# RWKV-5 attention with a SmeLU feed-forward on one core: another order of all steps, and the last copy in one piece

## The chip, the core and the metric

The kernel runs on one core of a Trainium2 chip. A core has five engines that run side by side and wait for one another by semaphores: TensorE (PE in the profile; its weight loads are listed as PEld), VectorE (DVE), ScalarE (ACT), GpSimd (POOL) and SyncE (SP), which here only issues DMAs. Transfers between the device's memory, the on-chip memory SBUF and again SBUF are carried by 16 DMA engines. Matmuls write into PSUM, a small memory of eight banks. The metric is the time of one execution in device microseconds. The kernel before took 175.04 us, the median of three runs (174.94 to 175.53).

## The reference

The first half is a linear attention with a decaying state, with batch 4, 8 heads, 768 steps and 48 columns per head; the second a feed-forward layer on 3072 tokens, 384 to 2048 to 384.

```python
for t in range(S):
    cur = einsum('bhd,bhe->bhde', u * k[t], v[t])
    y[t] = einsum('bhd,bhde->bhe', r[t], state + cur)
    state = w * state + einsum('bhd,bhe->bhde', k[t], v[t])
x = y.transpose(0, 2, 1, 3).reshape(B * S, H * D)
h = x @ w_in
g = where(h >= 1, h, where(h <= -1, 0, (h + 1) ** 2 / 4))
out = g @ w_out
```

## The kernel before

The 768 steps are cut into 6 chunks of 128. A unit n is one chunk of one batch row, 24 in all; a pair g holds units 2g and 2g+1, 12 in all. Within a chunk the recurrence is done by matmuls on scaled copies of K and R; from chunk to chunk a state of each batch row is carried on.

The steps for a pair g are these, each named as in the order below. `load.K.g`, `load.R.g` and `loadV.g` fetch inputs (SP; for g of 0 and 1 each in two halves, `.0` and `.1`). `V` casts V to bf16 (ACT). `Ks` and `Rs` scale K and R by powers of the decay, `KU` and `RKU` make the products for the u term, `usum` sums them per head, and `V2` scales V by that sum; most of these run on POOL. For the first three pairs `T` transposes Ks and Rs on PE and `TT` copies the result out of PSUM; for later pairs `KRT` transposes by DMA. `A` multiplies them, and `AT` masks A to the past. That is one masked product on DVE, or for two early units a cast on ACT and a mask on POOL. `Y` is the attention output (PE), and `y` adds V2 to it (DVE). `Sp` is a chunk's share of the state; `Tm` (DVE) adds the old state, `decay` (POOL) multiplies by the decay of a chunk, and `sbf` (ACT) makes a bf16 copy. `X` and `xT` transpose y: for the first three pairs on PE with a copy on ACT, later by DMA.

The feed-forward layer takes a pair's 256 tokens in four quarters q of 512 columns. `mm1.g.q` is 12 matmuls into a PSUM buffer h (three of these are shared with `A` and `T`). `relu` and `square` (ACT) and `gate` (DVE) compute the activation, and `mm2.g.j.q` is four matmuls that add unit j's share of that quarter into one of two PSUM banks. `o` copies the sum out, and `out` stores it. `w_in` (two pieces) and `w_out` (four) are weight loads that cast to bf16, issued by POOL on its own DMA queue.

What sets the order is one text, ORDER, written out by hand or by a search: a loop at the end of the kernel goes through its words, and each word issues one step. In `KU.0.1@D` the letter behind @ names the engine (D is DVE, P is POOL, A is ACT), and digits behind a colon name the buffers that the step takes. A number behind ~ puts so many idle matmuls ahead of a step, and `warm` is idle matmuls alone. Each engine runs its own instructions in the order of the text; SP's and POOL's DMA issues stand in theirs. A step that takes a buffer waits until its last reader is done. The line numbers of the profile that the text below uses: 210 copies and casts, 288 and 292 the weight loads, 302 the input loads, 325 Ks and Rs, 335 KU, 342 RKU, 367 V2, 404 A, 419 the mask, 444 Y, 479 decay, 516 mm1, 534 the gate, 544 mm2, 558 and 559 the last copy.

Of the kernel before, what the change touches and what calls it, by code (L numbers as in the profile page):

```python
# [43 lines left out]
relu.0.1:1 mm1.1.1.-1:0 gate.0.0:0 square.0.1:1 Tm.4@D:1 mm1.0.2.-1:2 relu.1.1:0 Y.5:1 square.1.1:0 V2.2.0@P:0 w_out.1
y.4:1 gate.0.1:1 w_out.2 X.4:0 w_out.3 mm1.0.3.-1:1 xT.4@A:2 gate.1.1:2 relu.0.2:1 Sp.3:0 y.5:2 mm1.1.0.-1:0
square.0.2:1 Tm.3@D KU.3.0@P:1 decay.4 gate.0.2:3 relu.0.3:0 relu.1.0:1 mm2.0.0.0:1 mm2.0.1.0:0 Ks.3.0@P:0 RKU.3.0@D:1
square.1.0:0 KRT.K.3:0 mm1.1.3.-1:2 mm2.0.1.1 Rs.3.0@P:0 mm2.0.0.1 square.0.3:1 gate.1.0:4 mm2.0.1.2 gate.0.3:5
# [580 lines left out]
```

## Time and profile before

| | |
|---|---|
| median of the runs | 175.04 us (174.94 to 175.53) |
| the profiled execution | 175.03 us, span 173.3 us |
| PE busy | 163.5 us, 94% |
| DVE, ACT busy | 134.8 and 134.9 us, 78% each |
| POOL busy | 118.1 us, 68% |
| share of the span on the last chain | PE 71%, DMA 10%, DVE 9%, ACT 5% |
| moved by DMA | 28.78 MB in 106,967 packets, most of them under 512 bytes |

The profile is one execution on the chip. Its parts are busy time by engine, the span in 40 slices, DMA queues (q1 has the transfers that SP issues, q0 those of POOL), the chain of work that ended last, groups of instructions with the idle time ahead of them and what ended it, and DMA issues with the time to landing. PE's busy time counts the depth of the pipeline, so a full PE is read from the idle time between instructions rather than from the share. Times are counted from the span's start.

### The profile page before, as it was taken

To read this page: it belongs to the slowest core of one execution; us is meant where nothing else is said; L and a number is where in the kernel's file an instruction comes from. 1 tells how busy PE (TensorE), PEld (TensorE's weight loads), DVE (VectorE), ACT (ScalarE), POOL (GpSimd) and SP (SyncE) were. 2 spreads that over 40 slices of the span, in tenths; PEclk is the share of its full clock that TensorE was granted. 3 is DMA by queue.
4 is the path that set the end of the run, shared out by engine and by line. 5 is a ranking of instruction groups with operands and counts; after the bars stand their busy time and mean duration, and the time that the engine had idled before them with its cause. 6 is when DMAs were issued, how large, how long until landed. Compare 5 with 4: busy or idle time off the path is not lost.

```text
span 173.3 us, 4141 instructions
## 1 busy us (share of the span) xinstructions
PE 163.5 (94%) x1674; PEld 123.7 (71%) x1674; DVE 134.8 (78%) x168; ACT 134.9 (78%) x194; POOL 118.1 (68%) x96
## 2 busy tenths in 40 slices
PE   7998789998999999979999999999999999999991
PEld 5786578765787866577786868876878868787650
...
GB/s 110 224 223 198 223 185 232 201 173 206 240 175 200 246 159 255 154 186 238 183 235 182 210 213 155 232 229 253 229 77 95 106 2 4 128 8 95 0 91 91
DMA packets 106967, 28.78 MB, mean 166 GB/s; under 512 B 100930, under 2 KB 106180, under 8 KB 106948
## 3 DMA queue, kind: packets, MB, share of 16 engines
...
q0 software_dynamic: 2912, 3.15, 11.3%
...
q14 instruction: 6, 0.05, 0.1%
...
## 4 chain that ended last, share of the span: by engine, by line
PE 71%; DMA 10%; DVE 9%; ACT 5%; issue 2%; POOL 1%; SPq 1%; DVEq 0%; POOLq 0%
PE hp L516 33%; PE op L544 30%; DMA VF<-in_v_dram 5%; DVE AT L419 3%; DMA xT<-yy 3%; PE A L404 3%; DVE RKU L342 2%; DMA K<-in_k_dram 2%; DVE gt L534 2%; PE Y L444 2%; PE Y L439 2%; PE Sp L430 1%; ACT V L210 1%; ACT RKU L353 1%; POOL V L367 1%
## 5 line engine op out<-in xcount | busy, mean ns | idle before, releaser
L516 PE MATMUL hp<-xT,w_in_sb 128*128 128x256 bf16 (+1 forms) x600 | 70.8, 268 | 2.7 <-DVE gt L534 1.0
L544 PE MATMUL op<-w_out_sb,gt 128*128 128x384 bf16 x384 | 71.7, 326 | 0.0
L534 DVE SCALAR_TENSOR_TENSOR gt<-sq,hp 128x1024 bf16<-128x1024 f32 x48 | 57.9, 1216 | 14.6 <-ACT sq L529 14.3
L516 PEld LDWEIGHTS <-w_in_sb 128*128 128x128 bf16 x600 | 55.8, 98 | 12.8 <-issue 2.9
L524 ACT ACTIVATE pt<-hp 128x1024 f32<-128x1024 f32 x48 | 48.6, 1017 | 13.5 <-PE hp L516 13.3
L529 ACT ACTIVATE sq<-pt 128x1024 f32<-128x1024 f32 x48 | 50.4, 1057 | 3.0 <-DVE gt L534 1.8
L544 PEld LDWEIGHTS <-gt 128*128 128x128 bf16 x384 | 35.6, 98 | 19.7 <-issue 0.2
L419 DVE TENSOR_TENSOR AT<-A,umask 128x1024 bf16<-128x1024 f32 x22 | 26.5, 1218 | 1.8 <-PE A L404 1.5
L367 POOL TENSOR_TENSOR V<-V,diag 128x768 f32<-128x768 bf16 (+1 forms) x12 | 16.5, 1375 | 9.1 <-ACT V L210 7.1
L335 POOL TENSOR_TENSOR KU<-K,u_bc 128x768 f32<-128x768 f32 (+1 forms) x13 | 21.3, 1640 | 1.9 <-DVE u_bc L210 1.8
L342 POOL TENSOR_TENSOR RKU<-R,KU 128x768 f32<-128x768 f32 (+1 forms) x13 | 20.7, 1595 | 0.3
L325 POOL TENSOR_TENSOR Ks<-Wdn,K 128x768 bf16<-128x768 f32 x10 | 18.3, 1828 | 2.1 <-PE Y L444 1.7
L479 POOL TENSOR_TENSOR state<-Tm,wCm 128x384 f32<-128x384 f32 x16 | 16.1, 1008 | 5.1 <-DVE Tm L466 5.1
L325 POOL TENSOR_TENSOR Rs<-Wup,R 128x768 bf16<-128x768 f32 x10 | 18.3, 1830 | 0.0
L458 DVE TENSOR_TENSOR yy<-Y,V 128x384 bf16<-128x384 f32 x18 | 9.9, 553 | 5.0 <-PE Y L444 3.5
L210 ACT CAST V<-VF 128x768 bf16<-128x768 f32 (+1 forms) x14 | 10.2, 736 | 2.7 <-DMA VF<-in_v_dram 2.7
L466 DVE TENSOR_TENSOR Tm<-Sp,state 128x384 f32<-128x384 f32 x16 | 8.9, 553 | 4.3 <-PE Sp L430 3.4
L444 PE MATMUL Y<-V,AT 128*128 128x48 bf16 x192 | 11.2, 184 | 1.1 <-POOL AT L414 0.7
L210 ACT COPY oo<-op 128x384 f32<-128x384 f32 x13 | 6.2, 475 | 7.6 <-PE op L544 7.5
L444 PEld LDWEIGHTS <-AT 128*128 128x128 bf16 x192 | 9.5, 96 | 2.7 <-POOL AT L414 1.0
L355 DVE TENSOR_REDUCE diag<-RKU 128x16 f32<-128x768 f32 (+1 forms) x13 | 11.0, 850 | 0.0
L210 ACT CAST state_bf<-state 128x384 bf16<-128x384 f32 x20 | 10.0, 504 | 0.0
...
## 6 DMA issues: line engine op xcount, KB each, us to landing
...
w_in_sb<-in_moe_w_in_dram POOLq DMA_DIRECT2D x2, 768.0 KB, 8.3
...
```

The lines of the kernel that those rows point to most:

```text
L210: nc.scalar.copy(out, in_) if e == "A" else engines[e].tensor_copy(out, in_)
L325: engines[e].tensor_mul(of_unit(dst, j0, j1)[:, :, :, :D], rep(tab, j1 - j0), of_unit(tiles[what, g], j0, j1))
L335: engines[e].tensor_mul(of_unit(tiles["KU", g], j0, j1), of_unit(tiles["K", g], j0, j1), rep(u_bc, j1 - j0))
L342: engines[e].tensor_mul(of_unit(tiles["RKU", g], j0, j1), of_unit(tiles["R", g], j0, j1), of_unit(tiles["KU", g], j0, j1))
L367: engines[e].tensor_mul(tiles["V2", g][:, hs, :], tiles["V", g][:, hs, :], tiles["diag", g][:, hs].unsqueeze(2).to_broadcast([P, hs.stop - ...
L419: nc.vector.tensor_mul(t.rearrange("p i n t -> p (i n) t"), tiles.pop(("A", n)).rearrange("p i n t -> p (i n) t"), umask.unsqueeze(1).to_b ...
L444: nc.tensor.matmul(t[:, 2 * p + i, :], tiles["AT", n][:, i, p, :], tiles["V", g][:, j * H + 2 * p + i, :], start=(c == 0), stop=True, skip ...
L516: nc.tensor.matmul(hp[:, f, cols], w_in_sb[:, i, n0 : n0 + P], tiles["xT", g][:, units, i, :], start=(i == 0), stop=(i == nK - 1), skip_gr ...
L524: nc.scalar.activation(tiles["pt", g, q], tiles["hp", g, q], AF.Relu, bias=0.5, scale=0.5)
L529: nc.scalar.activation(tiles["sq", g, q], tiles.pop(("pt", g, q)), AF.Square, bias=0.0)
L534: nc.vector.scalar_tensor_tensor(out=gt, in0=tiles.pop(("sq", g, q)), scalar=1.0, in1=tiles.pop(("hp", g, q)), op0=ALU.min, op1=ALU.max)
L544: nc.tensor.matmul(tiles["op", g, j], tiles["gt", g, q][:, f, j * P : (j + 1) * P], w_out_sb[:, n, :], start=(n == 0), stop=(n == nF - 1),)
```

## The change

All words of ORDER are put into another order, some with other engines, buffers and counts of idle matmuls. Those that change engines are u_bc, TT.2 and TT.4 (from DVE to ACT), usum.1.0 (ACT to DVE), KU.0.0 and KU.0.1 (exchanged between POOL and DVE), and nine of the copies o. The step `o` of the last unit copies its 384 columns on ACT in one piece; before, ACT copied 192 and DVE 192. Its store stays in two halves, on SP's queue and on ACT's. `W_OUT = 4` makes the number of pieces of w_out a constant with the slices it had, and `FUSE`, an empty list, adds a form of y that no pair takes.

The core of the diff, with the lines of ORDER that hold V.1.1, and those with w_in.0:

```diff
+W_OUT = 4
+FUSE = ()
...
-RKU.0.1@P T.2:2~9 TT.0@A:0 usum.0.0@D:0 Ks.1.1@D Ks.0.1@D KU.1.1@P Wup Sp.0:0 TT.2@D:1 A.0:1 V.0.1@A load.R.2.0:2
-AT.0.1:0 RKU.1.1@P Tm.0@D Sp.1:1~5 T.1:2 Tm.1@D w_in.0 V.1.0@A:1 A.2:1 Rs.1.1@D loadV.1.1 Sp.2:0 AT.0.0 TT.1@D:2
-usum.1.0@A:1 A.1:0~8 V2.0.0@P:0 Ks.2.0@P:2 AT.2.0:1 loadV.2.0:0 V2.1.0@A:1 Y.0:1 T.3:2 sbf.0@A Tm.2@D usum.0.1@D Y.2:0
...
-load.R.3.0:0 V.1.1@A X.1:1 Y.3:0 AT.5.0:0 A.4:0 V2.1.1@P xT.1@A mm1.0.0.1 V.2.0@A:2 Sp.5:1 y.3:0 RKU.2.0@P:0
...
+Rs.1.0@D:1 loadV.1.1 T.2:2 RKU.1.0@P:1 usum.0.0@D:0 Rs.0.1@D RKU.0.1@P V2.0.0@P:0 Tm.0@D V.1.0@A:1 Ks.0.1@D Ks.1.1@D
+A.0:1 Sp.2:0 KU.1.1@P TT.2@A:1 RKU.1.1@P Tm.2@D Rs.1.1@D usum.1.0@D:1 w_in.0 A.2:2 AT.2.0:0 sbf.0@A AT.0.1:1 AT.0.0
...
+Rs.2.0@P:2 y.0:0 Y.2:0 A.3:0 V.1.1@A Sp.3:1~4 V.0.1@A y.2:1 V2.0.1@A Sp.1:0 usum.1.1@D Tm.3@D warm.9.h.1 T.5:2 X.2:1
...
     def w_out_go(e, bk, i):
-        n = slice(i * FG, (i + 1) * FG)
+        n = slice(i * nF // W_OUT, (i + 1) * nF // W_OUT)
...
-            half = DO // 2
-            t = tiles["last", g, j] = [buf(bk[0], [P, half], F32, f"o_last{i}") for i in range(2)]
-            nc.scalar.copy(t[0], src[:, :half])
-            nc.vector.tensor_copy(t[1], src[:, half:])
+            t = tiles["last", g, j] = buf(bk[0], [P, DO], F32, "o_sb")
+            nc.scalar.copy(t, src)
...
-            for i, (queue, t) in enumerate(zip((nc.sync, nc.scalar), tiles.pop(("last", g, j)))):
-                queue.dma_start(out=rows[:, j, i * half : (i + 1) * half], in_=t)
+            t = tiles.pop(("last", g, j))
+            for i, queue in enumerate((nc.sync, nc.scalar)):
+                cols = slice(i * half, (i + 1) * half)
+                queue.dma_start(out=rows[:, j, cols], in_=t[:, cols])
```

Further on, the words from pair 4's A to its first mm1 read like this, before and after (other words left out): `A.9 A.8 mm2.2.1.2 mm2.3.0.0 mm2.2.1.3 mm2.3.0.1 Y.8 mm2.3.0.2 Y.9 mm2.3.0.3 A.11 A.10 mm2.3.1.0 Sp.10 mm2.3.1.1 mm2.3.1.2 Sp.9 mm2.3.1.3 mm1.4.0`, and now `A.9 A.8 mm2.2.0.2 mm2.2.1.1 mm2.2.0.3 mm2.2.1.2 mm1.3.1 Sp.8 mm2.2.1.3 mm1.3.2 Y.8 Y.9 mm1.3.3 mm2.3.0.0 mm2.3.1.0 mm2.3.0.1 mm2.3.1.1 mm2.3.0.2 A.11 A.10 mm2.3.0.3 mm1.4.0`. And `A.12 mm2.4.0.0 Sp.12 mm1.4.3` has become `A.12 mm1.4.2 mm2.4.0.0 Sp.12 mm1.4.3`. (The step numbers of mm2 are pair, unit and quarter.) POOL's steps from V2.3 to Rs.6 are the same in another order, with RKU.6 as one more: it stood behind Rs.6.

On ACT the casts of V at the start stood like this before. CAST V of 384 columns is a half (V.0.0, V.0.1, V.1.0, then V.1.1), the ACTIVATE of V with diag is V2 of a half, that of RKU is usum.1.0, and AT is the cast of A:

```order
L210 CAST V<-VF 128x384
L410 CAST AT<-A 128x1024
L210 CAST V<-VF 128x384
L353 ACTIVATE RKU,diag<-RKU 128x48 x8
L365 ACTIVATE V_340<-V,diag 128x48 x8
L210 CAST state_bf<-state 128x384
L410 CAST AT<-A 128x1024
L365 ACTIVATE V_333<-V,diag 128x48 x8
L210 COPY xT<-X 128x384 x2
L210 CAST state_bf<-state 128x384
L210 CAST V<-VF 128x384
L210 COPY xT<-X 128x384
```

Now, from the same place on, to the cast of V.2.0 (768 columns):

```order
L412 CAST AT<-A 128x1024
L367 ACTIVATE V_313<-V,diag 128x48 x8
L412 CAST AT<-A 128x1024
L212 CAST V<-VF 128x384 x2
L367 ACTIVATE V_249<-V,diag 128x48 x8
L212 COPY xT<-X 128x384 x2
L212 COPY TT<-T 128x1024
L212 CAST state_bf<-state 128x384
L212 COPY xT<-X 128x384
L212 CAST V<-VF 128x768
```

The two casts in one row are V.1.1 and V.0.1, in this order. They now stand ahead of V2 of the half 0.1, of the xT copies and of a copy TT; before, V.1.1 stood behind V2 of that half and two xT copies, and V.0.1 was the first row shown.

On POOL, around w_in.0 (the first DMA row), before:

```order
L342 TENSOR_TENSOR RKU<-R,KU 128x384 x2
L335 TENSOR_TENSOR KU<-K,u_bc 128x384
L342 TENSOR_TENSOR RKU<-R,KU 128x384
L288 DMA w_in_sb<-in_moe_w_in_dram 128x3x1024
L414 AFFINE_SELECT AT<-AT 128x1024
L367 TENSOR_TENSOR V_333<-V,diag 128x384
L325 TENSOR_TENSOR Ks<-Wdn,K 128x16x48
```

And now:

```order
L344 TENSOR_TENSOR RKU<-R,KU 128x384 x2
L369 TENSOR_TENSOR V_249<-V,diag 128x384
L337 TENSOR_TENSOR KU<-K,u_bc 128x384
L344 TENSOR_TENSOR RKU<-R,KU 128x384
L290 DMA w_in_sb<-in_moe_w_in_dram 128x3x1024
L416 AFFINE_SELECT AT<-AT 128x1024
L327 TENSOR_TENSOR Ks<-Wdn,K 128x16x48
```

V2.0.0 has moved from behind w_in.0 to ahead of it, and ahead of KU.1.1 and RKU.1.1.

On POOL, around Ks.3.0 (the first row with Ks; state is a decay step), before:

```order
L292 DMA w_out_sb<-in_moe_w_out_dram 128x4x384 x3
L335 TENSOR_TENSOR KU<-K,u_bc 128x768
L479 TENSOR_TENSOR state<-Tm,wCm 128x384
L325 TENSOR_TENSOR Ks<-Wdn,K 128x16x48
L325 TENSOR_TENSOR Rs<-Wup,R 128x16x48
L367 TENSOR_TENSOR V_863<-V,diag 128x768
```

And now:

```order
L294 DMA w_out_sb<-in_moe_w_out_dram 128x4x384 x2
L337 TENSOR_TENSOR KU<-K,u_bc 128x768
L294 DMA w_out_sb<-in_moe_w_out_dram 128x4x384
L327 TENSOR_TENSOR Ks<-Wdn,K 128x16x48
L489 TENSOR_TENSOR state<-Tm,wCm 128x384
L327 TENSOR_TENSOR Rs<-Wup,R 128x16x48
L489 TENSOR_TENSOR state<-Tm,wCm 128x384
L369 TENSOR_TENSOR V_865<-V,diag 128x768
```

decay.4 has moved from ahead of Ks.3.0 to behind it, and decay.5 from before V2.2.0 to behind Rs.3.0. RKU.3.0, which needs KU.3.0, stays on DVE between gate.0.2 and gate.1.0.

On SP the buffer of loadV.2.0 changes from the one that V.0.0 and V.0.1 read to the one that V.1.0 and V.1.1 read.

More of the change, by code (lines that the diff above doesn't have):

```diff
@@ L44 @@
[L44 to L47, printed above, removed]
-relu.1.3:1 loadV.3.0:1 mm2.0.0.2 mm1.1.2.-1:0 square.1.3:0 usum.3.0@D:1 mm2.0.0.3 relu.1.2:0 KRT.R.3:0 mm2.0.1.3
@@ L94 @@
[L94 to L97 removed]
+warm.18 load.K.0.0:0 load.R.0.0:0 load.K.0.1 load.R.0.1 load.K.1.0:1 load.R.1.0:1 bcu:0 lw loadV.0.0:0 loadV.0.1
@@ new lines @@
+mm2.4.0.1 xT.10:2 square.4.3:0 Sp.11:1 mm1.5.2.-1:1 gate.4.2:9 A.13:2 mm2.4.0.2 Tm.11@D:0 load.K.8.0:2 loadV.7.0:0
+out.2 Rs.7.0@P:1 KU.7.0@P:1 Y.12:1 sbf.9@A relu.5.2:0 RKU.7.0@P:1 gate.4.3:0 decay.12 AT.13.0:1 y.12:1 V.7.0@A:2
+square.5.2:1 mm2.4.0.3 mm1.5.0.-1:0 decay.11 load.R.8.0:2 out.3 o.4.0@A:0 Sp.13:1 relu.5.0:1 Ks.8.0@P:2 sbf.11@A
+mm1.5.1.-1:2 KRT.R.7:0 loadV.8.0:1 Tm.13@D:1 gate.5.2:1 KRT.K.8:1 mm2.4.1.0:0 KU.8.0@P:0 square.5.0:0 decay.13
+usum.7.0@D:1 relu.5.1:0 Rs.8.0@P:2 Y.13:1 mm2.4.1.1 mm2.4.1.2 y.13 Sp.14:1 gate.5.0:8 xT.12:1 square.5.1:1 mm2.4.1.3
@@ L98 @@
+relu.11.2:1 mm1.11.3.-1:1 gate.11.1:5 o.10.0@D:0 o.10.1@D square.11.2:1 mm2.11.1.0:1 mm2.11.0.0:0 out.10 out.9
+gate.11.2:0 mm2.11.1.1 mm2.11.0.1 mm2.11.1.2 mm2.11.0.2 relu.11.3:0 square.11.3:0 gate.11.3:7 mm2.11.1.3 o.11.1@D:0
+out.11.1 mm2.11.0.3 o.11.0@A:1 out.11.0
 """
```

117 lines of the change are left out of this document (61 added, 56 removed).

## The prediction

> **What bounds the kernel now.** I read the page first, then busy time by stretches of ten microseconds, then TensorE's waits, then the timeline at the places found. The page's first part and the stretches:
>
> ```profile
> PE 163.5 (94%) x1674; PEld 123.7 (71%) x1674; DVE 134.8 (78%) x168; ACT 134.9 (78%) x194; POOL 118.1 (68%) x96
> ...
> 30.00:40.00 10.00, 9.16 (x84) 6.76 (x83) 9.81 (x8) 8.16 (x10) 7.64 (x6) 1.00 1.31 189
> 40.00:50.00 10.00, 10.00 (x114) 7.61 (x112) 8.82 (x12) 8.53 (x12) 5.22 (x4) 1.00 1.24 217
> ```
>
> Each stretch has, after its length, busy time of PE, PEld, DVE, ACT and POOL, then granted clock, DMA share and GB/s. TensorE (PE) is the bound wherever it is full, and the work it is given is unchanged. The clock is 1.00 in both. So a new order can win or lose only where PE stands idle: in the first 40 us, at 74 and 81 us (rows below), and behind the last matmul. What ended PE's waits, with total, times and longest:
>
> ```profile
> PE hp L516 <- DVE gt L534: 1.0, 3, 0.6
> PE hp L516 <- DMA xT<-yy: 1.0, 1, 1.0
> ...
> PE hp L516 <- DVE AT L419: 0.4, 1, 0.4
> ```
>
> The profiled execution took 175.03 us, 173.3 of it span and 1.73 around it; the median of the runs is 175.04, so the sum is made on 175.03.
>
> **The start: the V loads and the first w_in load.** ScalarE (ACT) and GpSimd (POOL) in the timeline, and DMA before and after 16 us:
>
> ```profile
> 18.05 1.92 ACT L365 ACTIVATE V<-V,diag 128x48 f32<-128x48 bf16 x8
> 19.86 0.84 ACT L210 COPY xT<-X 128x384 bf16<-128x384 bf16 x2
> 20.59 0.53 ACT L210 CAST state_bf<-state 128x384 bf16<-128x384 f32 x1
> 22.24 0.51 ACT L210 CAST V<-VF 128x384 bf16<-128x384 f32 x1 [1.13 <-DMA VF<-in_v_dram]
> ...
> 23.63 0.83 ACT L210 CAST V<-VF 128x768 bf16<-128x768 f32 x1 [0.49 <-DMA VF<-in_v_dram]
> ```
>
> ```profile
> 12.94 0.93 POOL L288 DMA_DIRECT2D w_in_sb<-in_moe_w_in_dram  x1
> ...
> 14.94 0.84 POOL L367 TENSOR_TENSOR V<-V,diag 128x384 f32<-128x384 bf16 x1
> ...
> 20.31 0.80 POOL L288 DMA_DIRECT2D w_in_sb<-in_moe_w_in_dram  x1
> ```
>
> ```profile
> q1 hardware_dynamic: 15537, 2.94, 95.4%
> q0 software_dynamic: 37, 0.08, 3.8%
> ...
> w_in_sb<-in_moe_w_in_dram POOLq DMA_DIRECT2D x1, 768.0 KB, 8.5
> ```
>
> ```profile
> q0 software_dynamic: 176, 0.36, 101.4%
> q1 hardware_dynamic: 31, 0.01, 1.4%
> ```
>
> The third fence is 0 to 16 us, the fourth 16 to 18 us; q1 carries SP's loads, q0 POOL's weight loads. A load of one half (128 rows of 8 heads) is 1,024 packets, so by 16 us q1 had moved the 15 halves (15,360 packets) ahead of loadV.1.1, and then stood still while w_in.0 ran. That is why the cast V.1.1 (22.24) had to wait until w_in.0 had landed (12.94 + 8.5 = 21.4). Before, ACT did V2.0.1, two xT copies and a state cast in that time and lost 1.13 us. The next cast, V.2.0, waited 0.49 us for its own load.
>
> The change puts V.1.1 right behind AT.1.1 on ACT, which ended near 18.05 before (the first row begins there), ahead of V.0.1, V2.0.1, xT.2, xT.0, TT.4, sbf.1 and xT.1. Moreover loadV.2.0 now takes the buffer that V.1.1 reads, so SP cannot issue it until V.1.1 is done, and loads K.3 and R.3 stand behind it on SP. Against this, w_in.0 is issued later: V2.0.0 (0.84, the row at 14.94) now stands ahead of it on POOL, and loads K.1.1 and R.1.1, which POOL's steps ahead of it need, are one or two places later on SP. So w_in.0 moves by 0.8 to 1.1 us. q1 moves 2.94 MB in about 14 us, so the 0.19 MB of a half takes 0.9 us: loadV.1.1 just fits ahead of w_in.0, if its descriptors are there when R.2.0's end.
>
> If it fits, V.1.1 starts near 18, V.2.0's load is issued near 18.5 and lands behind w_in.0 (22.2 to 22.5) by its 1.7 us, about 23.9 against 23.6; ACT's seven steps end by then too. I count this as 0.0, with 0.5 both ways. That is the value I take, since w_in.0's shift is at least nearly what the half needs. That usum.1.0 leaves ACT for DVE, and TT.2, TT.4 and u_bc come to ACT, lies inside this: in either order ACT ends this stage waiting for a load.
>
> **RKU.3.0 on DVE behind POOL.** This is the wait that PE feels at 39.65:
>
> ```profile
> 33.08 1.03 POOL L479 TENSOR_TENSOR state<-Tm,wCm 128x384 f32<-128x384 f32 x1
> 34.03 1.85 POOL L325 TENSOR_TENSOR Ks<-Wdn,K 128x768 bf16<-128x768 f32 x1
> 35.80 1.84 POOL L325 TENSOR_TENSOR Rs<-Wup,R 128x768 bf16<-128x768 f32 x1
> ```
>
> ```profile
> 34.32 4.15 DVE L342 TENSOR_TENSOR RKU<-R,KU 128x768 f32<-128x768 f32 x1
> ```
>
> ```profile
> 39.65 1.47 PE L516 MATMUL hp<-xT,w_in_sb 128*128 128x256 bf16 x12 [0.64 <-DVE gt L534]
> ```
>
> RKU.3.0 began at 34.32 while Ks.3.0 ran, and ended at 38.47, 0.83 us after Rs.3.0 did (37.64): it stood until POOL had a pause. The gate behind it then released PE. Now POOL does Ks.3.0, decay.4, Rs.3.0, decay.5 without a pause, where decay.5 was done at 25.5 and decay.4 stood ahead of Ks.3.0. Of the two only decay.5 is new on POOL's way from KU.3.0 to its pause: the pause comes later by 1.0 (the decay's row), plus 0.2, an estimate, because usum.2.0, for which V2.2.0 on POOL waits, now stands behind two Tm steps on DVE. PE already waits there, so the whole 1.2 us is paid. The bounds: 0.64 below nothing (RKU.3.0 slips in ahead of Ks.3.0, and PE's wait at 39.65 is gone), and 2.2 above (both decays come late). I take +1.2, since the only row of this kind shows DVE losing to back-to-back POOL steps.
>
> The Trainium skill, "SBUF — State Buffer", section "SBUF: two separate sides", says that a DVE operation with two inputs in SBUF and a GpSimd operation that reads SBUF share a port pair as an exclusive lock, held for a whole instruction by whichever starts first. The 4.15 us row agrees with a lock and not with a split bandwidth; by the same rule RKU.3.0 would take 0.83 us if it came first, which is the second rival below.
>
> **The middle.** From the chain what a piece of mm2, a group of mm1, y.9 and the transpose of xT take, then PE's other two waits and the groups of ACT's transposed copy and DVE's mask:
>
> ```profile
> 47.09 0.65 PE op L544 x4
> 47.73 1.31 PE hp L516 x12
> ...
> 69.44 0.56 DVE yy L458
> 70.02 4.57 DMA xT<-yy
> ```
>
> ```profile
> 74.63 1.47 PE L516 MATMUL hp<-xT,w_in_sb 128*128 128x256 bf16 x12 [0.98 <-DMA xT<-yy]
> ...
> 79.57 0.40 PE L404 MATMUL A<-RT,KT 48*128 48x128 bf16 x8
> ...
> 81.29 0.92 PE L516 MATMUL hp<-xT,w_in_sb 128*128 128x256 bf16 x7 [0.39 <-DVE AT L419]
> ```
>
> ```profile
> L419 DVE TENSOR_TENSOR AT<-A,umask 128x1024 bf16<-128x1024 f32 x22 | 26.5, 1218 | 1.8 <-PE A L404 1.5
> ...
> L210 ACT COPY TT<-T 128x1024 bf16<-128x1024 bf16 x1 | 1.0, 1013 | 0.0
> ```
>
> Between Y.9 and mm1.4.0 stood five pieces of mm2 (0.65 each), two A and two Sp: 4.15 us of PE work, where y.9 and the transpose need 0.56 + 4.57. Now there are mm1.3.3 (1.31), six pieces and two A: 5.8 us. The 0.98 goes. Between A.12 and mm1.4.3, which takes A.12's PSUM buffer, stood 0.8 us of work; now mm1.4.2 is there as well, 2.1 us, and the mask (1.2 us) fits. The 0.39 goes. Late next is A.12 itself, for which Rs.6 must be scaled on POOL and transposed by DMA:
>
> ```profile
> 44.78 1.48 POOL L367 TENSOR_TENSOR V<-V,diag 128x768 f32<-128x768 bf16 x1 [7.13 <-ACT V L210]
> ...
> 68.47 1.85 POOL L325 TENSOR_TENSOR Rs<-Wup,R 128x768 bf16<-128x768 f32 x1
> ```
>
> ```profile
> RT<-Rs SPq DMA_TRANSPOSE x9, 4.6
> ```
>
> POOL stays full behind the first of these rows. From there to Rs.6 it now has one step more, RKU.6, as long as Rs.6 itself: Rs.6 ends about 1.8 us later than the 70.3 of before, near 72.1. A.12 comes 1.5 us of PE work (a group of mm1 and a Sp) and those two waits earlier than 79.57, near 76.7. So 4.6 us are left for a transpose of 4.6. I charge 0.3, between 0 and 1.3. The middle brings 0.98 + 0.39 - 0.3 = 1.1.
>
> **The end.** The last copy of before, and what one piece costs:
>
> ```profile
> 169.81 0.32 ACT L558 COPY o_last<-op 128x192 f32<-128x192 f32 x1 [3.09 <-PE op L544]
> 170.16 0.36 DVE L559 COPY o_last<-op 128x192 f32<-128x192 f32 x1 [0.44 <-ACT o_last L558]
> ...
> 170.56 0.38 ACTq L577 DMA_DIRECT2D out_dram<-o_last  x1
> ```
>
> ```profile
> L210 ACT COPY oo<-op 128x384 f32<-128x384 f32 x13 | 6.2, 475 | 7.6 <-PE op L544 7.5
> ```
>
> The two halves ran one behind the other and the last store was issued at 170.56. One copy of 0.475 ends at 170.29, so both stores start about then: -0.25. The bounds are 0 (the stores' landing sets the end) and -0.3.
>
> The other moves (nine o copies between ACT and DVE, three more idle matmuls in PE's pauses at the start, W_OUT and FUSE, which change no instruction) I cost at nothing: the copies lie under PE, which is full there; if that cover went, an o copy on ACT is the 0.475 us above. The sum is 175.03 + 0.0 + 1.2 - 1.1 - 0.25 = **174.9 us**, with 173.8 to 176.0 as this case's own range.
>
> **The rivals.**
>
> First, slower: loadV.1.1 does not get ahead of w_in.0. It decides at one point, whether its packets run before w_in.0's. Then V.1.1 starts at 22.24 as before, and the seven steps behind it on ACT come after: with V.1.1 itself 0.51 + 0.51 + 1.92 + 0.84 + 1.01 + 0.53 + 0.42 (xT.1, half of the pair's row) = 5.7, less the overlaps of neighbours 5.3, so V.2.0 cannot start before 27.5, against 23.63: +3.9. Its load is issued only at 22.8 and then meets w_in.1 (issued at 20.31, under way for 8.5 us as w_in.0 was, so to 28.8), behind which its 1.7 us end near 30.1 at the earliest of that kind: +6.5. I take +5.0, between the two; ACT feeds PE from there until 40 us, so PE pays it, with the 1.2 of RKU.3.0, less 1.1 and 0.25: 175.03 + 5.0 + 1.2 - 1.1 - 0.25 = 179.9, and 178.8 to 181.4 by the two ends. For it speaks that V.1.1 waited exactly this way before; against it the later w_in.0.
>
> Second, faster: all as forecast, but RKU.3.0 finds POOL's port free. PE's wait of 0.64 us at 39.65 goes instead of growing: 175.03 - 0.64 - 1.1 - 0.25 = 173.0. POOL's w_out.3 between KU.3.0 and Ks.3.0 speaks for it, a shift of 0.3 us decides (34.03 against 34.32); the row of before speaks against.
>
> Third: A.12, or a transpose behind it, is late in the middle, since POOL has no pause to catch up in; nothing of the 1.1 is gained: 175.03 + 1.2 - 0.25 = 176.0.
>
> **How the numbers follow.** The forecast 0.38, late V.1.1 0.35, free port 0.12, full POOL 0.15. What a measurement here can tell from no change is about 0.3%, 0.5 us: faster is below 174.5, slower above 175.6. The forecast's range gives 0.16 faster, 0.17 same, 0.05 slower; with the rivals 0.29 faster (0.12 of it the free port, 0.01 the full POOL), 0.19 same, 0.52 slower. The range 172.9 to 180.3 leaves out about half of the free-port case and the worst third of the late one, under 0.2.
>
> **What would show it.** In the changed kernel's profile: the idle time that a DMA of VF ends ahead of ACT's casts (over 3 us at the third half cast: the first rival); the first 128x1024 relu on ACT near 24.5 (forecast) or near 29; DVE's RKU at 5 us or more, or below 1 (second rival), and PE's wait for the gate at 39 to 42; no PE wait for xT at 74; a PE wait ahead of an A near 77 (third); the last two stores issued within 0.1 us. I am wrong if the loads of the first 25 us come in another order than SP and POOL issue them, or if PE finds waits between 90 and 165 us, where none of the three waits above lies.

## The result, and the profile after

The changed kernel takes 180.08 us (median of four runs, 179.72 to 181.51), beside 175.17 us (median of four) for the kernel before: a ratio of 1.030 with a 95% interval of 1.025 to 1.035. It is slower, by about 5 us; the forecast of 174.9 us was wrong in sign, and the time is the one that the first rival gave (179.9). The profiled execution took 180.22 us, its span is 178.5 us against 173.3. Here and below a ratio leaves out executions more than 1.5% above the fastest of their kernel, and for four kernels whose executions fell apart by several us the times are given instead.

In the changed kernel's profile the lines are numbered 2 higher up to Y and 10 higher from y on: 212 copies and casts, 304 the input loads, 327 Ks and Rs, 344 RKU, 489 decay, 526 mm1, 534 now the relu, 544 now the gate, 554 mm2. The first part of the page, and PE's longest waits (total, times, longest):

```profile
PE 164.3 (92%) x1677; PEld 125.8 (71%) x1677; DVE 132.8 (74%) x166; ACT 135.9 (76%) x180; POOL 118.9 (67%) x96
```

```profile
PE Sp L432 <- ACT V L212: 5.5, 3, 4.7
PE hp L526 <- DVE gt L544: 1.5, 2, 1.1
PE A L406 <- DMA RT<-Rs: 1.2, 1, 1.2
```

PE's work is the same (164.3 us busy against 163.5); what was added is above all one wait of 4.7 us for a cast of V on ACT. The waits for xT and for AT of the kernel before are gone, and one for RT has come. The two stretches in which that wait lies, and the second of them in the kernel before (PE was busy for 8.73 us in the first), with the granted clock in the third column from the end:

```profile
10.00:20.00 10.00, 6.09 (x110) 4.92 (x109) 7.32 (x14) 6.30 (x14) 9.46 (x9) 1.00 1.07 193
20.00:30.00 10.00, 7.21 (x101) 6.71 (x101) 5.07 (x8) 6.27 (x16) 6.42 (x6) 0.66 1.05 178
```

```profile
20.00:30.00 10.00, 8.65 (x137) 7.28 (x135) 8.79 (x13) 8.31 (x13) 9.66 (x10) 1.00 1.19 215
```

ACT, PE, POOL, DVE and SP's DMA issues in the timeline of the changed kernel:

```profile
21.80 0.92 ACT L212 CAST V<-VF 128x384 bf16<-128x384 f32 x2 [4.07 <-DMA VF<-in_v_dram]
...
29.29 0.83 ACT L212 CAST V<-VF 128x768 bf16<-128x768 f32 x1 [0.45 <-DMA VF<-in_v_dram]
...
30.40 1.03 ACT L534 ACTIVATE pt<-hp 128x1024 f32<-128x1024 f32 x1
```

```profile
15.16 0.39 PE L388 MATMUL T<-ident,Rs 128*128 128x128 bf16 x4
...
22.37 0.89 PE L432 MATMUL Sp<-V,Ks 128*128 128x96 bf16 x8 [4.72 <-ACT V L212]
...
24.01 0.63 PE L388 MATMUL T<-ident,Ks 128*128 128x128 bf16 x4
...
45.11 1.47 PE L526 MATMUL hp<-xT,w_in_sb 128*128 128x256 bf16 x12 [1.13 <-DVE gt L544]
...
83.23 0.40 PE L406 MATMUL A<-RT,KT 48*128 48x128 bf16 x8 [1.16 <-DMA RT<-Rs]
```

```profile
13.88 0.93 POOL L290 DMA_DIRECT2D w_in_sb<-in_moe_w_in_dram  x1
...
41.29 1.81 POOL L327 TENSOR_TENSOR Rs<-Wup,R 128x768 bf16<-128x768 f32 x1
43.07 1.71 POOL L489 TENSOR_TENSOR state<-Tm,wCm 128x384 f32<-128x384 f32 x1
```

```profile
39.69 4.24 DVE L344 TENSOR_TENSOR RKU<-R,KU 128x768 f32<-128x768 f32 x1
```

```profile
13.06 9.64 SPq L304 DMA_DIRECT2D VF<-in_v_dram  x2
```

The V loads on SP and the first relu in the kernel before:

```profile
12.63 3.34 SPq L302 DMA_DIRECT2D VF<-in_v_dram  x2
```

```profile
24.36 1.02 ACT L524 ACTIVATE pt<-hp 128x1024 f32<-128x1024 f32 x1
```

The packets of 16 to 18 us in the changed kernel, SP's queue (q1) and POOL's (q0):

```profile
q0 software_dynamic: 139, 0.28, 98.8%
q1 hardware_dynamic: 51, 0.01, 2.4%
```

Read together: w_in.0 was issued 0.94 us later than before (13.88 against 12.94), but SP came to issue loadV.1.1 later too (13.06 against 12.63). Between 16 and 18 us SP's queue moved 51 packets beside 139 of w_in.0, so loadV.1.1 stood still again, and V.1.1 could start only at 21.80. Now seven steps stand behind it on ACT, and Sp.3 on PE, which idled 4.72 us. V.2.0 came at 29.29 (before: 23.63), the first 128x1024 relu at 30.40 (24.36), the group of mm1 that waits for the gate at 45.11 (39.65): 5.5 us late. To the last copy 0.4 us of that is recovered (174.87 against 169.81, below).

### The profile page after: what moved, and what is told of

Read it like the earlier page. It is cut to its first block, busy times and chain, and to the rows that moved or that the text cites. A ratio compares the mean times of both kernels' runs of the same rounds, so it can differ in the third digit from the quotient of the medians.

```text
span 178.5 us, 4132 instructions
## 1 busy us (share of the span) xinstructions
PE 164.3 (92%) x1677; PEld 125.8 (71%) x1677; DVE 132.8 (74%) x166; ACT 135.9 (76%) x180; POOL 118.9 (67%) x96
## 3 DMA queue, kind: packets, MB, share of 16 engines
HBM read 20.45 MB, written 4.72 MB: 141 GB/s over the span
## 4 chain that ended last, share of the span: by engine, by line
PE 52%; DMA 15%; POOL 11%; ACT 8%; SPq 7%; DVE 2%; issue 2%; POOLq 0%; DVEq 0%
PE op L554 24%; PE hp L526 23%; DMA VF<-in_v_dram 9%; SPq L304 7%; ACT pt L534 4%; DMA K<-in_k_dram 4%; POOL Rs L327 3%; ACT sq L539 3%; DMA RT<-Rs 2%; POOL RKU L344 2%; POOL KU L337 2%; POOL Ks L327 2%; DVE gt L544 2%; PE A L406 2%; POOL state L489 2%
## 5 line engine op out<-in xcount | busy, mean ns | idle before, releaser
L554 PE MATMUL op<-w_out_sb,gt 128*128 128x384 bf16 x384 | 70.5, 326 | 0.0
L489 POOL TENSOR_TENSOR state<-Tm,wCm 128x384 f32<-128x384 f32 x16 | 16.6, 1048 | 0.7 <-DVE Tm L476 0.7
L432 PE MATMUL Sp<-V,Ks 128*128 128x96 bf16 x80 | 6.8, 214 | 5.5 <-ACT V L212 5.5
L357 DVE TENSOR_REDUCE diag<-RKU 128x16 f32<-128x768 f32 (+1 forms) x14 | 11.6, 830 | 0.0
L432 PEld LDWEIGHTS <-Ks 128*128 128x128 bf16 x80 | 5.7, 103 | 6.7 <-issue 5.7
```

What stands on the lines that cost most here:

```text
L489: nc.gpsimd.tensor_mul(states[(g % BP) * UNITS + j], tiles.pop(("Tm", n)), wCm)
L554: nc.tensor.matmul(tiles["op", g, j], tiles["gt", g, q][:, f, j * P : (j + 1) * P], w_out_sb[:, n, :], start=(n == 0), stop=(n == nF - 1),)
```

## The experiments

The expectations are quoted as they stood before each run. Names such as V.1.1 and RKU.3.0 are the words of ORDER.

### Which half of the order

Both orders have issued exactly the same steps at one point, behind load.R.4.0 and V.3.0, near 46 us (idle matmuls aside). So the halves can be joined crosswise at this seam.

```diff
 old_start: ORDER before, up to "xT.5@A V.3.0@A:3" (with Ks.3.0@P:1 and loadV.3.0:0)
          + ORDER changed, from "sbf.5@A sbf.2@A sbf.3@A mm1.2.3.-1:1" on, square:0 and square:1 exchanged
 new_start: ORDER changed, up to "V.3.0@A:3 load.R.4.0:1" (with loadV.3.0:1)
          + ORDER before, from "mm1.2.3.-1:1 gate.1.2:7 sbf.3@A" on, square:0 and square:1 exchanged
```

> The order of the kernel before up to load.R.4.0 and V.3.0 (where both orders have issued the same steps, near 46 us), and the order of the changed kernel from there to the end, with its last copy in one piece. Three buffer numbers are fitted to the seam: Ks.3.0 and loadV.3.0 take those of the changed kernel, and the two buffers of square are exchanged behind the seam. Theory (all the loss lies in the start, and the changed middle gains little): PE's wait for a gate at 39.65 stays at 0.6, the waits for xT at 74 and AT at 81 are gone, one wait of 0.8 to 1.5 us for RT near 77 takes their place; ratio to before 0.997 to 1.002. The prediction's sum for this part is -1.1 -0.25, a ratio of 0.992. Rival (the changed order is slower behind the seam as well): ratio above 1.005.

> The other half: the order of the changed kernel up to the same seam, and that of the kernel before from there on, with its last copy in two pieces (loadV.3.0 takes the other buffer, the two of square are exchanged behind the seam). Theory: PE's wait for V.1.1 of 4 to 5 us and the one for a gate of about 1 us as in the changed kernel, and those for xT and AT of before (1.4 us together) in the middle: ratio 1.028 to 1.036. Rival: below 1.02.

Measured: old_start 0.9989 of the kernel before (0.9958 to 1.002). new_start's six runs went from 177.95 to 183.27 us, median 180.96, beside 175.68 for the kernel before; the profiled one took 180.6. PE's waits in old_start, then in new_start:

```profile
PE A L406 <- DMA RT<-Rs: 1.7, 1, 1.7
```

```profile
PE Sp L430 <- ACT V L210: 5.4, 2, 4.7
PE hp L516 <- DVE gt L534: 1.5, 2, 1.1
...
PE hp L516 <- DMA xT<-yy: 0.9, 1, 0.9
PE hp L516 <- DVE AT L419: 0.4, 1, 0.4
```

So the loss is in the first 46 us. Behind the seam the changed order is worth nothing either way: it takes away the waits for xT and AT (1.4 us) and pays 1.7 us for RT.

### The one move suspected, put into the kernel before

```diff
-sbf.0@A ... AT.1.1:2 ... V2.0.1@A ... xT.2@A:0 ... xT.0@A:1 sbf.1@A ... load.R.3.0:0 V.1.1@A
+sbf.0@A ... AT.1.1:2 ... V.1.1@A V2.0.1@A ... xT.2@A:0 ... xT.0@A:1 sbf.1@A ... load.R.3.0:0
```

> The kernel before with one word moved: V.1.1 stands right behind AT.1.1 on ACT, ahead of V2.0.1, the copies xT.2 and xT.0, sbf.1 and xT.1, as in the changed kernel; w_in.0, the V loads and their buffers stay. First rival of the prediction, its first half alone: V.1.1 still starts near 22.2, ACT idles some 4 us ahead of it, V.2.0 and the first relu come 3.4 to 3.9 us later (relu at 27.8 to 28.3), total plus 3 to 4, ratio 1.016 to 1.023. Rival (ACT's order alone is covered by other work, and the loss needs loadV.2.0's buffer too): first relu below 26, ratio below 1.008.

Measured: 1.0245 (1.0196 to 1.0294), 179.74 us beside 175.35. ACT's casts and first relu, and the stretch of 20 to 30 us:

```profile
22.55 0.51 ACT L210 CAST V<-VF 128x384 bf16<-128x384 f32 x1 [3.77 <-DMA VF<-in_v_dram]
...
29.86 1.02 ACT L524 ACTIVATE pt<-hp 128x1024 f32<-128x1024 f32 x1 [0.60 <-PE hp L516]
```

```profile
20.00:30.00 10.00, 5.25 (x76) 4.65 (x74) 3.99 (x6) 4.81 (x15) 5.80 (x5) 0.66 1.15 213
```

One word moved makes the kernel before 4.3 us slower, an amount near the whole loss. The relu comes 5.5 us late, not 3.4 to 3.9: PE, which waits for the copies xT behind V.1.1, idles 4.7 us, and afterwards its clock is down to 0.66 in this stretch. The rival, that loadV.2.0's buffer is needed too, is out.

### loadV.1.1 let ahead of w_in.0

```diff
-RKU.1.1@P ... usum.1.0@D:1 w_in.0 A.2:2 AT.2.0:0 sbf.0@A AT.0.1:1 AT.0.0
+RKU.1.1@P ... usum.1.0@D:1 A.2:2 AT.2.0:0 sbf.0@A AT.0.1:1 AT.0.0 w_in.0
```

> The changed kernel with one word moved: w_in.0 stands behind POOL's mask AT.0.0 (1.10 us) instead of ahead of it, so it is issued near 15.0 us instead of 13.88. Theory (the meeting of two queues decides: loadV.1.1's packets stand still because w_in.0's run): loadV.1.1 now gets ahead, V.1.1 starts at 17.7 to 19, PE's wait of 4.72 us for it falls below 1.5, the first 128x1024 relu moves from 30.40 to 24.5 to 26, total 175 to 176.5. Rival (1.1 us is still too little, q1's ring is that far behind): V.1.1 lands behind w_in.0, thus 1.1 later than before, and the total goes up to 181.

In the profile the theory holds. Packets of 16 to 18 us, then ACT:

```profile
q0 software_dynamic: 32, 0.07, 51.0%
q1 hardware_dynamic: 730, 0.14, 35.5%
```

```profile
18.14 0.92 ACT L212 CAST V<-VF 128x384 bf16<-128x384 f32 x2 [0.65 <-DMA VF<-in_v_dram]
...
25.18 1.03 ACT L534 ACTIVATE pt<-hp 128x1024 f32<-128x1024 f32 x1
```

Yet the kernel is hardly faster: 178.39 to 181.66 us, ratio 1.0232 (1.0174 to 1.0291), an interval that overlaps with the changed kernel's. A second stall stood behind the first. POOL, DVE and PE of the same run:

```profile
33.09 1.81 POOL L337 TENSOR_TENSOR KU<-K,u_bc 128x768 f32<-128x768 f32 x1 [2.02 <-DMA K<-in_k_dram]
...
40.18 0.98 POOL L489 TENSOR_TENSOR state<-Tm,wCm 128x384 f32<-128x384 f32 x1
```

```profile
36.66 5.32 DVE L344 TENSOR_TENSOR RKU<-R,KU 128x768 f32<-128x768 f32 x1 [2.11 <-DMA R<-in_r_dram]
```

```profile
43.17 1.47 PE L526 MATMUL hp<-xT,w_in_sb 128*128 128x256 bf16 x12 [2.89 <-DVE gt L544]
```

Loads K.3.0 and R.3.0 came late, RKU.3.0 started late on DVE and then stood until POOL's last step was done (it ended at 36.66 + 5.32 = 41.98, 0.82 us behind that step's end at 41.16), and PE waited 2.89 us for the gate behind it. The group of mm1 that started at 39.65 in the kernel before starts at 43.17.

### The start mended further

start_mended also issues loadV.2.0, K.3.0 and R.3.0 about as early as before the change:

```diff
 (as win_later, and)
-V2.1.0@A:1 ... V.1.1@A Sp.3:1~4 V.0.1@A ... KU.2.0@P:0 loadV.2.0:1 xT.1@A
+V2.1.0@A:1 V.0.1@A loadV.2.0:0 ... V.1.1@A Sp.3:1~4 ... KU.2.0@P:0 xT.1@A
 (loadV.3.0 and on: buffers 0 and 1 exchanged)
```

> The changed kernel with its start mended at three places: w_in.0 behind POOL's mask AT.0.0 (as in win_later), V.0.1 behind V2.1.0 on ACT, where ACT idled for 0.96 us, and loadV.2.0 in the buffer that V.0.1 frees, so that loads K.3.0 and R.3.0 behind it on SP are issued near 16 to 18 us instead of 22 to 27. Theory now (two stalls lie behind one another: V.1.1's, and behind it K.3.0's and R.3.0's loads and RKU.3.0 on DVE against POOL's unbroken steps): first relu near 25, KU.3.0 on POOL without a wait for K, but RKU.3.0 still ends 0.83 us after the last of POOL's four steps, PE's longest wait for a gate 1.0 to 2.5, total 176 to 178. Rival (the prediction's sum was right once V.1.1 is early: RKU costs 1.2): total 174.5 to 175.5.

Measured: 179.19 us, 1.0175 (1.0099 to 1.0251), above both expectations. SP issued K.3.0 at 16.91, and KU.3.0 still waited 2.00 us for it (start 32.91). What holds K.3.0 up is the weight load w_out.0, which the changed order puts ahead of RKU.2.0 on POOL: it was issued at 23.97 here, at 26.46 in the kernel before. With w_out.0 behind RKU.2.0 (start_rku_middle, below) KU.3.0 starts at 31.97 without a wait; in start_rku_pool, its neighbour without that move, it waits 1.25 us and starts at 33.75. In the four profiles that have w_out.0 ahead and K.3.0 issued near 17 us the wait was 0.8 to 2.0 us.

Two kernels undo the place of V.1.1 instead. v11_back puts it behind xT.1 again, with Sp.3, Y.3, V2.1.1, Tm.3, y.3 and loadV.2.0 behind it; v11_and_buffer_back also gives loadV.2.0 the buffer of before.

```diff
 v11_back:
-V.1.1@A Sp.3:1~4 ... Tm.3@D ... Y.3:0 ... V2.1.1@P ... y.3:1 ... loadV.2.0:1 xT.1@A
+xT.1@A V.1.1@A Sp.3:1~4 Y.3:0 V2.1.1@P Tm.3@D y.3:1 loadV.2.0:1
 v11_and_buffer_back, moreover:
-V2.0.1@A ... y.3:1 loadV.2.0:1
+V.0.1@A loadV.2.0:0 V2.0.1@A ... y.3:1   (loadV.3.0 and on: buffers exchanged)
```

> The changed kernel with V.1.1 put back behind ACT's copy xT.1, and Sp.3, Y.3, V2.1.1, Tm.3 and y.3, which need it, behind it; loadV.2.0 still takes V.1.1's buffer. Theory (two locks: ACT's and PE's order, and the buffer): PE's wait of 4.72 is gone, TensorE's clock stays up in 20 to 30 us, but V.2.0's load is still issued only at about 22.8 and lands near 28.8, so the first relu starts at 29.5 to 30.4 and the total falls by at most 1: 179 to 180. Rival (the place of V.1.1 in ACT's order alone is the cause): the first relu starts near 24.5 and the total is 174.5 to 175.5.

> The same, and loadV.2.0 takes the buffer of V.0.0 and V.0.1 as before the change (V.0.1 stands ahead of V2.0.1 on ACT), and is issued right behind loadV.1.1. Theory: V.1.1 still starts near 22.2, nobody on PE waits for it, V.2.0's load lands near 23.6, the first relu starts at 24.4 to 25.5, total 174.4 to 175.6. Rival (the rest of the new order of the start costs something too): first relu later than 26, total above 176.

v11_back takes 184.84 us (1.0529, 1.0492 to 1.0565), the slowest kernel whose executions agree, against my expectation of a small gain. SP's issue of the two V loads, and ACT:

```profile
13.02 12.05 SPq L304 DMA_DIRECT2D VF<-in_v_dram  x2
```

```profile
24.16 0.52 ACT L212 CAST V<-VF 128x384 bf16<-128x384 f32 x1
33.15 0.83 ACT L212 CAST V<-VF 128x768 bf16<-128x768 f32 x1 [8.47 <-DMA VF<-in_v_dram]
```

V.1.1 ran 2.4 us later than in the changed kernel, so V.2.0's load was issued 2.4 us later (the issues end at 25.07, in the changed kernel at 22.70), and it landed 4 us later. That it waited behind more of the weight loads is likely but not shown. The shared buffer is thus a second lock with a price of its own, which V.1.1's place in the changed order hid. With the buffer undone as well it takes 178.25 to 181.52 us (1.0211, 1.0148 to 1.0275): V.2.0 no longer waits, but RKU.3.0 takes 5.72 us (36.29 to 42.01) with its loads in time, and PE waits 2.62 us for the gate. The rival expectation of above 176 came true.

### TensorE's clock after the stall

```diff
-V.1.1@A Sp.3:1~4
+V.1.1@A Sp.3:1~74
```

> The changed kernel with 74 idle matmuls ahead of Sp.3 instead of 4, so that TensorE is busy from 17.3 to 22.1 while it waits for V.1.1; nothing else moves. Theory A (the granted clock of 0.66 in 20 to 30 us comes from the 4.7 us of idling, and it costs time): clock 1.00 there, the transposes T at 0.39 us for four instead of 0.63, the copies xT 1 to 2 us earlier, total down by 0.5 to 1.5. Theory B (V.2.0's load, which lands at 28.84 whatever PE does, covers it): clock 1.00, but the first relu stays within 0.4 us of 30.40 and the total falls by less than 0.4.

SP's issue of the V loads, and ACT:

```profile
12.66 8.79 SPq L304 DMA_DIRECT2D VF<-in_v_dram  x2
```

```profile
20.55 0.93 ACT L212 CAST V<-VF 128x384 bf16<-128x384 f32 x2 [2.79 <-DMA VF<-in_v_dram]
```

Inconclusive for the price. The clock in 20 to 30 us was 0.95 instead of 0.66 and V.1.1 came at 20.55, but V.2.0's load, issued 1.25 us earlier than in the changed kernel (its issue ends at 21.45 against 22.70), landed later: ACT cast it at 31.55, after idling 5.53 us for it, against 29.29. PE idled 5.36 us for it, and the clock of 30 to 40 us was 0.71. The kernel took 182.03 us (1.0363, 1.0323 to 1.0403). What the lower clock costs by itself stays open; that V.2.0's load sets this stage whatever PE does, as theory B had it, fits, but not that the time would stay.

### RKU.3.0 against POOL

changed_rku and start_and_rku move RKU.3.0 one gate earlier on DVE, in the changed kernel and in start_mended; start_rku_rs6 also puts Rs.6 ahead of RKU.6.

```diff
-gate.0.2:3 mm1.0.3.-1:1 ... relu.0.3:1 RKU.3.0@D:1 square.0.3:1 ... gate.1.0:4
+RKU.3.0@D:1 gate.0.2:3 mm1.0.3.-1:1 ... relu.0.3:1 square.0.3:1 ... gate.1.0:4
 start_rku_rs6, moreover:
-RKU.6.0@P:0 ... loadV.6.0:1 ... Rs.6.0@P:0 ... KRT.R.6:1
+Rs.6.0@P:0 KRT.R.6:1 RKU.6.0@P:0 ... loadV.6.0:1
```

> The changed kernel with RKU.3.0 ahead of gate.0.2 on DVE, and nothing else. POOL issues w_out.3 from 37.73 to 38.53 there, and DVE is idle for 0.73 us before 38.56. Theory (lock by the first to start): RKU.3.0 takes 0.8 to 1.0 us, PE's wait of 1.13 us for the gate at 45.11 falls below 0.3, total 179.0 to 179.6. Rival: RKU.3.0 above 2.5 us and the total unchanged.

> As start_mended, and RKU.3.0 one gate earlier on DVE, ahead of gate.0.2, so that it can start while POOL issues w_out.3 and before POOL starts Ks.3.0. Theory (whichever starts first keeps the other out): RKU.3.0 takes 0.8 to 1.0 us instead of 4 to 5, PE's wait for a gate near 40 falls below 0.4, total 1 to 2 us under start_mended. Rival (the two share bandwidth, or POOL wins anyway): RKU.3.0 stays above 2.5 us.

> As start_and_rku, and Rs.6 ahead of RKU.6 on POOL (its DMA transpose right behind it on SP, ahead of loadV.6.0), as before the change. Theory (PE's wait of 1.16 us for RT near 82 is Rs.6 come too late): that wait falls below 0.3, and the total is 0.6 to 1.2 under start_and_rku. Rival (the wait moves to what RKU.6 feeds, usum.6 and y of units 12 and 13): another wait of about 1 us between 85 and 100, same total.

changed_rku: RKU.3.0 took 1.26 us (37.92), PE's longest wait for a gate fell from 1.13 to 0.4, and the ratio was 1.0206 (1.0143 to 1.0269). This interval overlaps with the changed kernel's, so whether the 0.7 us reach the total is open. Ks.3.0, which started 0.74 us behind RKU.3.0, took 2.20 us here instead of 1.82. start_and_rku and start_rku_rs6 differ in nothing up to 60 us, and show the two ways in which the same place can go. DVE and POOL in start_and_rku, then in start_rku_rs6:

```profile
34.95 0.96 DVE L344 TENSOR_TENSOR RKU<-R,KU 128x768 f32<-128x768 f32 x1 [1.34 <-POOL KU L337]
```

```profile
35.70 1.90 POOL L327 TENSOR_TENSOR Ks<-Wdn,K 128x768 bf16<-128x768 f32 x1
```

```profile
34.97 7.02 DVE L344 TENSOR_TENSOR RKU<-R,KU 128x768 f32<-128x768 f32 x1 [1.98 <-POOL KU L337]
```

```profile
35.71 1.82 POOL L327 TENSOR_TENSOR Ks<-Wdn,K 128x768 bf16<-128x768 f32 x1
...
40.19 0.98 POOL L489 TENSOR_TENSOR state<-Tm,wCm 128x384 f32<-128x384 f32 x1
```

With the same gap of 0.7 us before Ks.3.0, RKU.3.0 once ran in 0.96 us and once stood through all four POOL steps, to 0.8 us after the last (41.99), though it started before them in both. PE's longest wait for a gate was 1.2 us in the first and 7.9 us in the second, 6.7 of the 8.6 us between the two executions. The runs of start_and_rku were 176.66, 181.4, 186.71 and 189.15 us, those of start_rku_rs6 176.91, 185.22, 185.29 and 186.41; the profiles are of the 176.66 and the 185.29. That all the long ones are of this kind is not shown.

start_rku_pool takes RKU.3.0 off DVE; start_rku_middle also moves w_out.0 behind RKU.2.0 and Rs.6 ahead of RKU.6; before_decays and before_rku_pool ask the same of the kernel before.

```diff
 start_rku_pool, before_rku_pool:
-RKU.3.0@D:1
+(behind Ks.3.0) RKU.3.0@P:1
 start_rku_middle, moreover:
-w_out.0 A.4:2 ... RKU.2.0@P:0
+A.4:2 ... RKU.2.0@P:0 w_out.0
 before_decays (the kernel before):
-decay.5 ... decay.4 gate.0.2:3 ... Ks.3.0@P:0 ... Rs.3.0@P:0
+gate.0.2:3 ... Ks.3.0@P:0 decay.4 ... Rs.3.0@P:0 decay.5
```

> As start_mended, but RKU.3.0 is made by POOL, behind Ks.3.0, instead of by DVE, so that DVE has no instruction there that needs POOL's pause. Theory (in start_and_rku one and the same program ran RKU.3.0 once in 0.96 us, and in start_rku_rs6 the same place took 7.02 us: who starts first is decided by under 0.1 us, and the loser waits for POOL's last step): no wait for a gate above 0.4 us on PE at 40, executions that agree within 1.5 us, total 175 to 176.5. Rival (POOL's 1.82 us more make Rs.3.0 and V2.3.0 late): a PE wait of 1 us or more between 45 and 60 for A or y, total 177 or more.

> As start_rku_pool, and two more: w_out.0 is issued behind RKU.2.0 on POOL, so that loads K.3.0 and R.3.0 have 1.8 us more of the DMA engines to themselves, and Rs.6 stands ahead of RKU.6 as before the change. Theory (all the waits named so far, and nothing else, made the changed kernel slow): KU.3.0 waits less than 0.5 us for K, PE's wait for RT near 80 below 0.3, total 173.8 to 175.0, thus not slower than the kernel before. Rival (the middle of the changed order is no better than the old one): waits of 1 us or more in 75 to 95, total 175.5 or more.

> The kernel before, with decay.4 behind Ks.3.0 and decay.5 behind Rs.3.0 on POOL, as in the changed kernel. Prediction's step (RKU.3.0 on DVE waits for POOL's pause): RKU.3.0 starts near 34.3 and ends 0.83 us after decay.5, near 39.4 to 39.7, PE's wait for the gate grows from 0.64 to 1.5 to 1.9, total plus 0.9 to 1.2. Rival (as in the changed kernel's trace, DVE gets in ahead of decay.5): RKU.3.0 ends at 38.5, total within 0.3.

> The kernel before with RKU.3.0 on POOL, behind Ks.3.0, instead of on DVE. Theory (the 4.15 us of RKU.3.0 on DVE are waiting for POOL, and they are what holds the gate back): DVE is free, PE's wait of 0.64 us for the gate at 39.65 is gone, Rs.3.0 1.8 us later without a wait on PE for its transpose: ratio 0.995 to 0.998. Rival (the 1.8 us of POOL come back as a wait for RT or V2 in 45 to 90 us): ratio 1.000 or more.

start_rku_pool: 1.0117 (1.0072 to 1.0162). No wait for a gate is left, but PE waits 2.7 us for RT in two places. start_rku_middle: 177.57, 177.72, 184.02 and 184.52 us; K.3.0 is in time, the wait for RT is gone, and 1.5 us for a copy on ACT and 1.5 us for a gate between 75 and 85 us stand there instead. So each wait named could be taken away, and with all of them the best runs are 177.6, still above the kernel before (176.31 there): the rival came true, and the expectation of 173.8 to 175.0 was wrong. For start_rku_pool the rival came true in the time alone; its wait was to lie between 45 and 60 us, and the two for RT lie at 80 and 104.

before_decays: 1.0004 (0.9964 to 1.0045). R.3.0 came at 38.4 us in this execution, and DVE and POOL then wanted it at once:

```profile
38.42 0.96 DVE L342 TENSOR_TENSOR RKU<-R,KU 128x768 f32<-128x768 f32 x1 [2.40 <-DMA R<-in_r_dram]
```

```profile
38.46 2.60 POOL L325 TENSOR_TENSOR Rs<-Wup,R 128x768 bf16<-128x768 f32 x1 [1.79 <-DMA R<-in_r_dram]
```

DVE started 0.04 us sooner and took 0.96; Rs.3.0 took 2.60 instead of 1.84. Neither the forecast of 0.9 to 1.2 us nor its rival's row (an end at 38.5) shows, but the time is the rival's. With R.3.0 this late, the profile doesn't show the case that was asked about. before_rku_pool: 0.9972 (0.9946 to 0.9998), PE's wait of 0.64 for the gate gone: faster than the kernel before by about 0.5 us, with an interval that just leaves out no change.

### The middle, with the old start

```diff
 old_start_rs6 (old_start, and):
-RKU.6.0@P:0 decay.7 ... decay.8 ... Rs.6.0@P:0 A.11:0 usum.6.0@D:0 A.10:1 V2.5.0@P:1 ... Tm.9@D:1
+decay.7 ... decay.8 ... Rs.6.0@P:0 A.11:0 A.10:1 V2.5.0@P:1 RKU.6.0@P:0 ... Tm.9@D:1 usum.6.0@D:0
 old_start_rs6_rku_pool, moreover: RKU.3.0@P:1 behind Ks.3.0
```

> As old_start, and RKU.6 moved on POOL from ahead of decay.7 to behind V2.5 (its usum.6 on DVE behind Tm.9), so that Rs.6 ends 1.8 us earlier, near 72.0. Theory (of the changed middle nothing but the late Rs.6 eats the gain): PE's wait of 1.67 us for RT at 78.59 falls below 0.3, ratio to before 0.990 to 0.995. Rival (POOL has no pause, so something else is late): another wait of 1 us or more in 75 to 95, ratio 0.996 to 1.002.

> As old_start_rs6, and RKU.3.0 on POOL behind Ks.3.0 as in before_rku_pool. Both theories together: ratio 0.988 to 0.995, not above old_start_rs6 by more than 0.002. Rival (POOL's 1.8 us are missing further on): above old_start_rs6 by 0.003 or more.

Measured 0.9977 (0.9947 to 1.0006) and 0.9961 (0.9929 to 0.9992). PE's waits in the middle, of the first, then of the second:

```profile
PE A L406 <- DMA RT<-Rs: 0.8, 1, 0.8
...
PE Sp L432 <- DVE oo L212: 0.3, 1, 0.3
```

```profile
PE Sp L432 <- DVE oo L212: 0.8, 1, 0.8
...
PE A L406 <- DMA RT<-Rs: 0.2, 1, 0.2
```

The wait for RT shrinks from 1.7 to 0.8 and 0.2, and one for a copy on DVE grows in its place. About 1 us stays in sum: nearer the first rival's reading than the theory's, though no single wait of 1 us is left. The second kernel missed its ratio of at most 0.995 too, but POOL's 1.8 us were not missing further on either. It is faster than both kernels, by 0.4% against the kernel before (0.1% to 0.7%), the lowest ratio of these experiments; its interval overlaps with before_rku_pool's, so what the changed middle adds to that is not shown.

### The last copy alone

```diff
-            t = tiles["last", g, j] = [buf(bk[0], [P, half], F32, f"o_last{i}") for i in range(2)]
-            nc.scalar.copy(t[0], src[:, :half])
-            nc.vector.tensor_copy(t[1], src[:, half:])
+            t = tiles["last", g, j] = buf(bk[0], [P, DO], F32, "o_sb")
+            nc.scalar.copy(t, src)
```

> The kernel before, with the last copy alone changed: 384 columns on ACT in one piece, the stores as in the changed kernel. Prediction: 0.25 us less (bounds 0 and 0.3). Rival (the stores' landing sets the end): both stores issued within 0.1 us of one another, the span unchanged within 0.1 us.

Measured 1.0012 (0.9974 to 1.005). The end of the changed kernel (span 178.5), then of this one (span 174.8):

```profile
174.87 0.48 ACT L567 COPY o_sb<-op 128x384 f32<-128x384 f32 x1 [3.09 <-PE op L554]
175.37 0.34 SPq L587 DMA_DIRECT2D out_dram<-o_sb  x1
175.38 0.38 ACTq L587 DMA_DIRECT2D out_dram<-o_sb  x1
```

```profile
171.15 0.48 ACT L557 COPY o_sb<-op 128x384 f32<-128x384 f32 x1 [3.09 <-PE op L544]
```

Both stores are issued together as forecast, 0.5 us behind the copy's start where the last one was 0.75 behind. But from that start to the span's end it is 3.63 and 3.65 us, and it was 3.49 with two pieces, so these profiles show no gain. That the stores' landing sets the end fits, but no row shows it; the ratio, uncertain by 0.4%, is too coarse for 0.25 us.

## Why the prediction was wrong, and where it was right

**The start: wrong, by 5 us; this is the failed step.** It took 0.0 because "w_in.0's shift is at least nearly what the half needs": 0.8 to 1.1 us of shift against 0.9 for a half at the mean rate. w_in.0's issue did move by 0.94. But the issue of loadV.1.1 was taken as fixed, and it moved by 0.43 (13.06 against 12.63), because the issue of R.2.0 ahead of it took longer; so the net shift was 0.5. And the 0.9 was too small a need. In two profiles with the same order of SP and POOL here the net shift was as large as the forecast wanted: 0.94 in idle_for_clock (V loads at 12.66, w_in.0 at 13.91), where V.1.1 came at 20.55, and 1.06 in changed_rku (12.69 and 14.06), where it came at 22.18. A net shift of 1.4 us was enough in start_and_rku (13.69 and 15.40, V.1.1 at 18.40 without a wait), as were the 2.3 of win_later (12.72 and 15.29). What happens between 1.06 and 1.4 no run shows. The first rival's chain of steps held row by row: V.1.1 at 21.80 (22.24 foretold), V.2.0's load issued at 22.7 (22.8), V.2.0 at 29.29 between its ends of 27.5 and 30.1 (28.8 and 1.7 make 30.5, not 30.1). That its total of 179.9 so nearly met 180.08 is in part luck: with RKU.3.0 it put +6.2 at the mm1 of 45.11, which came 5.5 late, and it took off 1.35 for the middle and the end, which gave 0.3. before_v11_early shows that V.1.1's place makes 4.3 us in the order of before; in the changed order it hides a second stall of nearly the same price, as follows.

**The forecast's own case would not have come true either.** win_later comes close to that case: V.1.1 at 18.14, first relu at 25.18. None of its executions is below 178.39 us, where 174.9 was forecast. Missed was that loads K.3.0 and R.3.0, which the text saw "behind it on SP", have users: KU.3.0 and RKU.3.0 waited 2.0 and 2.1 us. Missed altogether was w_out.0, which moved ahead of RKU.2.0 on POOL and runs into those loads.

**RKU.3.0: the wait came, but not until POOL's pause.** The term was +1.2, by POOL's pause coming later. In the changed kernel RKU.3.0 did not stand until that pause. It ended 0.83 us after Rs.3.0, as before, and decay.5 was the one that stood (1.71 us instead of 1.0): the extra decay cost nothing, and PE's wait grew by 0.5 (1.13 against 0.64). In win_later and start_rku_rs6 the same instruction stood to the end of the last decay (5.32 and 7.02). Who starts first keeps the other out, which is how the Trainium skill's page "SBUF — State Buffer", section "SBUF: two separate sides", has it. The rows of before_decays (DVE 0.96 us, POOL's step 2.60) and changed_rku (1.26 and 2.20) agree; the row of 7.02 us agrees with a lock, but not with its going to the first by the profile's times, since RKU.3.0 started 0.74 us before Ks.3.0 and still came last. So with gaps of 0.7 us the outcome differs from one execution to the next, and the +1.2 has no single price in its place.

**The middle: the two waits went, and the third rival took the gain.** The 0.98 and the 0.39 are gone as worked out. Charged was 0.3 us for A.12, between 0 and 1.3; it was 1.16 in the changed kernel and 1.67 with the old start, where the forecast of this part (-1.1) measured 0.9989 together with the end. Rs.6 ended at 78.8 for an A that PE reached at 82.1, 3.3 us where 4.6 were forecast. The reason given, that POOL has no pause to catch up in, is only part of it. Counted from V2.3's start, Rs.6 ended 28.6 us later (50.18 and 78.81) where it was 25.5 before: 1.8 of the 3.1 us are RKU.6, as forecast, and 0.98 are a wait of Ks.6 for load K.6 on POOL (1.10 with the old start), which the prediction did not have.

**The end: -0.25 was 0 as far as the profiles show**, the bound that was named and not taken.
